# Two of four steps of the first unit's first matrix product in seven products instead of eight

## The chip, the cores and the metric

The kernel runs on one core of one Trainium2 chip. The time is device microseconds of that core, from the first to the last instruction of the program. Five engines work from queues of their own: TensorE (PE, with its weight loads as PEld), VectorE (DVE), ScalarE (ACT), GpSimd (POOL) and SyncE (SP), which mostly issues transfers.

## The reference

```python
kv  = einsum('bhsd,bhse->bhde', k, v)            # 8 batches, 8 heads, 576 rows, 64 columns
out = einsum('bhsd,bhde->bhse', q, kv)
x   = out / sqrt(mean(out**2, -1) + 1e-6) * g_norm   # put together as 4608 x 512
h   = x @ w_in                                   # w_in 512 x 2048
g   = s * max(h, 0)**2 + b
return g @ w_out                                 # w_out 2048 x 512
```

Everything but the two weights is float32. The weights arrive as 64-bit floats and are turned into float32 on the chip.

## The kernel before

The 4608 rows of `x` are worked through in nine **units** of 512 rows. A unit has a first stage (`h` and `g`, called mm1) and a second (`g @ w_out`, called mm2). The attention that makes the `x` of the next unit runs beside them.

**Seven products.** The 2048 columns of `w_in` are taken in four **steps** of 512. Within a step the product of a 512x512 weight block and the unit's 512 columns of `x` transposed is a product of two 2x2 block matrices. Taken plainly it is eight block products. By Winograd's form of Strassen's scheme it is seven, at the price of sums: four of the blocks of `w_in` (`sums_w_in`, two calls `s12` and `s34`, result in `ws`, one in place in `wb`), four of the blocks of `x` (`x_sums`, result in `xs`, shared by all steps of a unit), and additions of the products. `mm1(u, s)` does one step so. The products are named by the PSUM bank and a number: `x1`, `z2`, `x6`, `y7`, `x5`, `x3`, `y4`. `x1`, `x6`, `x5` and `x3` go one after the other into the same bank, each added to what is there. So before `x6` starts, the bank must have been copied out (`keep("r1", ...)`, a ScalarE copy), before `x5` again (`r2`), before `x3` again (`r4`). `z2` plus `r1` is the block `a11` of `h`, `y7` plus `r4` is `a22`, `y4` plus `r2` is `a12`, `x3` gives `a21`. Each is rectified and squared on VectorE (`relu_sq`) and then scaled by `s` and shifted by `b` on ScalarE (`affine`); `a21` is done on ScalarE alone.

**The first unit** takes all four steps plainly (`mm1_plain`, line 656): four slots to a step, each a block of `h` made by eight matmuls of 128x256, into PSUM banks `x` and `y` in turn, two buffers each. `out_of` rectifies the bank's content into a tile of `g` and squares it; the scaling waits in the list `to_scale`, and `scale_g` puts it on ScalarE's queue later. `first_unit` (line 1624) runs the 16 slots; slots 0 to 3 are step 0, and so on. `slots0[0]` and `slots0[1]` are run earlier, between the last pieces of the first attention.

**The conversion of the weights** lies beside these slots. There are 16 tiles: 0 to 7 are `w_in`, 8 to 11 the upper half of `w_out` (`w_up`), 12 to 15 the lower (`w_dn`). A tile comes by DMA into one of three buffers (`w_raw`), takes two passes on ScalarE (`hi`, line 225, and `lo`, line 230) and two on VectorE (`shift`, line 235, and `plus`, line 245). The dictionary `tile_at` says after which slot which tile is converted, `more_at` after which slot a piece of the differences of `w_out`'s halves is formed (`sub_w_out(5, 5, 1, ...)`). All 16 are done by the last slot.

**The second stage of the first unit** is also in seven products, with one difference: product 5 is taken early (`early_5`), with `s1`, the sum of `a21` and `a22` (`g_s1`). Its slots are `x1(0)`, `x1(1)`, `early_5(0)`, `early_5(1)`, `z2(0)`, `z2(1)`, `x6(0)`, and so on; a slot is eight matmuls of 128x256 over the eight blocks of `w_out`, and `z2` is the first that reads `w_dn`. Hung on these slots are: sums of `g` in place (`s2`, `t3`, `s4`), the difference `w_t2` of the halves of `w_out`, the stores of `w_out`'s parts for the later units (`store_w2`), and the load of the next keys, values and queries (`load_kv`, `loads`). The keys and values of batch 1 and `w_t2` go into the three buffers that the weight tiles leave.

**Order.** The order of the instructions on each engine is the order of the program text: nothing is moved by a scheduler. Each engine works through its queue in turn and waits, by semaphores, for operands and for buffers to come free.

Of the kernel before, what the change touches and what calls it, by code (L numbers as in the profile page):

```python
# [16 lines left out]
def kernel(  # L17
# [628 lines left out]
    def relu_sq(t, last=True):  # L646
        nc.vector.scalar_tensor_tensor(t, t, 0.0, t, ALU.max, ALU.mult)  # L647
        if last:
            affine(t)
# [57 lines left out]
    def mm1(u, s):  # L707

        st = {}

        def keep(name, src, tag):
            st[name] = rp.tile([P, 2, TB], FP32, name=name, tag=tag)
            nc.scalar.copy(st[name], src)  # L713

        def x1():
            st["x"] = bank_of("x", "x")
            mm1_product(1, u, s, st["x"], True)
            keep("r1", st["x"], "ra")

        def z2():  # L720
            ps = bank_of("z", "z", 1)
            mm1_product(2, u, s, ps, True)
            t = g_tile("a11", s)
            add(t, ps, st["r1"])
            relu_sq(t)

        def x6():
            mm1_product(6, u, s, st["x"], False)
            keep("r2", st["x"], "rb")

        def y7():
            st["y"] = bank_of("y", "y")
            mm1_product(7, u, s, st["y"], True)

        def x5():
            mm1_product(5, u, s, st["x"], False)
            keep("r4", st["x"], "ra")
            t = g_tile("a22", s)
            add(t, st["y"], st["r4"])
            relu_sq(t)  # L740

        def x3():
            mm1_product(3, u, s, st["x"], False)
            relu_sq_on_act(g_tile("a21", s), st["x"])

        def x3_s1():
            g_tile("s1", s)
            g_s1(s)

        def x3_s3():  # L750
            sub(ga["a21", s], ga["a11", s], ga["a21", s])

        def y4():
            mm1_product(4, u, s, st["y"], False)
            add(g_tile("a12", s), st["y"], st["r2"])

        def y4_square():
            relu_sq(ga["a12", s])

        return dict(  # L760
            x1=x1, z2=z2, x6=x6, y7=y7, x5=x5, x3=x3, x3_s1=x3_s1, x3_s3=x3_s3, y4=y4, y4_square=y4_square,
        )

# [299 lines left out]
    def mm2(u, step=None, side={}):  # L1063
# [148 lines left out]
        def x1(j):  # L1212
            st["x", j] = half(("x", j), "x")
            product(1, j, st["x", j], True)
            part("r1", j, st["x", j])

        def early_5(j):

            ps = half(("w", j), "y")
            product(5, j, ps, True)  # L1220
            nc.scalar.copy(rows("o1", j)[:, HN:], ps)
# [41 lines left out]
        def seq(fn, *more):  # L1263
            def run():
                fn()
                for m in more:
                    m()
            return run
# [11 lines left out]
        if u == 0:  # L1280
            return [
                lambda: x1(0),
                seq(lambda: x1(1), s2),
                lambda: early_5(0),
                lambda: early_5(1),
                lambda: z2(0),
                seq(lambda: z2(1), t3),
                lambda: x6(0),
                seq(lambda: x6(1), s4, t4),
                lambda: y7(0),  # L1290
                lambda: y7(1),
                lambda: x3(0),
                lambda: x3(1),
                lambda: y4(0),
                lambda: y4(1),
            ]
# [231 lines left out]
    gp = ctx.enter_context(tc.tile_pool(name="gp", bufs=NS // 2))  # L1528


    slots0 = [slot for s in range(NS) for slot in mm1_plain(s)]
    turn[0]()
    turn[1]()
    take[0]()
# [82 lines left out]
            for load in load_q(4 * u + 2 * i):  # L1617
                load()  # L1618

    tile_at = {1: 3, 2: 4, 3: 5, 4: 6, 5: 7, 6: 8, 7: 9, 9: 10, 10: 11, 11: 12, 12: 13, 14: 14, 15: 15}  # L1620
    more_at = {8: 8, 9: 9, 12: 10, 13: 11, 14: 12, 15: 13}

    def first_unit():
        for n, slot in enumerate(slots0):
            if n > 1:
                out_of = slot()
                if out_of:
                    out_of()
                if n % 4 == 0:
                    g_s1(n // 4 - 1)  # L1630
            if n in tile_at:
                for step in (hi, lo, shift, plus):
                    step(tile_at[n])
            scale_g()
            if n in more_at:
                more(more_at[n])
        g_s1(NS - 1)

    def x3(a):
        a["x3"]()  # L1640
# [5 lines left out]
    def sides(u, A, B):  # L1646

        first, second = {}, {}  # L1650
        kv = []
        if u in kv_due:
            kv.append(lambda: kv_product(kv_due[u], u > 2))
            kv.append(lambda: used(*((u, "kv", (n, m)) for n in range(NP) for m in range(2))))
        q = {half: [partial(loads, u + 2, half)] for half in range(2)}
        if u == 1:
            for s in range(1, NS):
                first[((0, 1), (0, 3), (1, 1))[s - 1]] = list(sums_w_in(s))
            first.update({
                (1, 3): kv,  # L1660
                (2, 0): [partial(A["turn"], 0), partial(A["turn"], 1)],
                (2, 1): [A["product"]],
                (2, 2): [A["back"]],
                (2, 3): [A["square"]],
                (3, 0): [A["row_sum"]],
                (3, 2): [A["norm"], A["turn_x"]],
                (3, 3): [lambda: [load() for load in load_q(12, rest_on=nc.sync)]],
            })
            return first, second
        if u + 1 == U:  # L1670
            return first, second
        if u == 2:
            first = {
                4: [A["turn"]],
                5: kv,
                8: [A["product"]],
                9: [A["back"], B["turn"]],
                10: [A["square"]],
                11: [A["row_sum"]],
                12: [B["product"]],  # L1680
                13: [A["norm"]],
                14: [A["turn_x"]],
                15: [B["back"], *q[0]],
            }
            second = {
                0: [B["square"]], 1: [B["row_sum"], A["scale"]], 2: [B["norm"]], 3: [B["turn_x"], *q[1]],
                "sums": [B["scale"]],
            }
        else:
            first = {  # L1690
                2: [A["turn"]],
                4: [A["product"], *kv],
                5: [A["back"]],
                6: [A["square"], B["turn"]],
                7: [A["row_sum"]],
                8: [A["norm"]],
                9: [A["turn_x"]],
                10: [B["product"], *q[0]],
                11: [B["back"], A["scale"]],
                12: [B["square"]],  # L1700
                13: [B["row_sum"]],
                14: [B["norm"]],
                15: [B["turn_x"], *q[1]],
            }
            second = {1: [B["scale"]]}
        second[5], second[6] = [[lambda n=n: x_sums(u + 1)[n]()] for n in range(2)]
        return first, second

    for u in range(U):
        A, B = pairs_of(u + 1) if u + 1 < U else (None, None)  # L1710
        if u == 0:
            first_unit()
            second = mm2(0)
        else:
            if u == 1:
                loads(2, 0)
                loads(2, 1)
            first, at_second = sides(u, A, B)
            if u > 1:
                run, last = mm1_deep(u)  # L1720
                second = mm2(u, last, at_second)
                run(lambda n: [fn() for fn in first.get(n, [])], second["early"])
                second["rest"]()
                continue
            steps = [mm1(u, s) for s in range(NS)]
            second = mm2(u)
# [21 lines left out]
        for n, slot in enumerate(second):  # L1748
            slot()
            if u == 0:  # L1750
                if n == 1:
                    for i in range(2):
                        load_kv(1, i, convp, tag="raw", bufs=3)
                    store_w2(1)
                    loads(1, 0)
                    loads(1, 1)
                    store_w2(5)
                elif n == 2:
                    t2 = convp.tile([P, 4 * R * D], FP32, name="w_t2", tag="raw", bufs=3)
                    W2_AT[6] = t2[:, : FC // 2 * HN].rearrange("p (f n) -> p f n", n=HN)  # L1760
                    for i in range(14, 16):
                        more(i)
                    sub_w_out(6, 3, 5)
                    store_w2(3, 2, 6)
            if n == 0 and u > 0:
                x3(steps[-1])
                y4(steps[-1])
            for step in side.get(n, []):
                step()
# [33 lines left out]
```

## Time and profile before

| | |
|---|---|
| time, median of 3 runs | 910.12 us (910.0 to 910.18) |
| profiled span | 908.9 us, TensorE clock 1.000 |
| VectorE, ScalarE, GpSimd busy | 664.5, 356.0, 228.1 us |
| first slots of the first unit | 23.86 us |
| end of its slot 7, start of slot 8 | 53.16 us |
| end of its slot 15, start of `x1(0)` | 80.79 us |
| start of `x6(0)` | 101.51 us |
| start of unit 1 | 135.96 us |

The first unit as busy time of each engine, in stretches of 10 us (PE, PEld, DVE, ACT and POOL with the number of instructions, then the granted clock, the share of the DMA engines and GB/s):

```profile
40.00:50.00 10.00, 10.00 (x48) 8.81 (x47) 8.61 (x12) 8.80 (x11) 0.00 (x0) 1.00 1.01 341
50.00:60.00 10.00, 10.00 (x48) 8.81 (x47) 9.31 (x13) 9.41 (x12) 0.00 (x0) 1.00 0.97 338
60.00:70.00 10.00, 10.00 (x49) 8.79 (x47) 9.66 (x14) 9.37 (x11) 0.00 (x0) 1.00 0.77 258
70.00:80.00 10.00, 10.00 (x48) 8.81 (x47) 8.34 (x12) 7.12 (x9) 0.00 (x0) 1.00 0.88 319
80.00:90.00 10.00, 10.00 (x48) 8.81 (x47) 9.06 (x13) 4.45 (x7) 0.00 (x0) 1.00 0.76 226
90.00:100.00 10.00, 10.00 (x48) 8.79 (x47) 1.42 (x3) 0.74 (x2) 0.00 (x0) 1.00 0.93 243
```

A float32 matmul shows as two records, so a slot of eight matmuls has 16. In a timeline the columns are start, length of the piece, engine, line, operation, output and inputs, shape, number, and in brackets the idle time before it with its releaser. Pieces overlap a little, since the end of one instruction runs into the next.

### The profile page before, as it was taken

The numbers are of one execution on the slowest core, as the hardware profiler recorded it, in microseconds if no ns is written. First come the engines' busy times: TensorE is split into PE (matmuls) and PEld (weight loads), VectorE is DVE, ScalarE is ACT, GpSimd is POOL, SyncE is SP. The second block draws the span as 40 slices with busy tenths as digits, with TensorE's granted clock in tenths as the row PEclk, the third lists the DMA queues.
The fourth block names the chain that finished last, engine by engine and source line by source line (L and its number), as shares of the span: only waits on it lengthen the run. The fifth ranks groups of instructions, "written<-read, shape, count | busy, mean of one in ns | idle before, by whom it ended". The sixth has DMA issues, their size and how long they took to land.

```text
span 908.9 us, 19257 instructions
## 1 busy us (share of the span) xinstructions
PE 897.7 (99%) x7522; PEld 825.3 (91%) x7522; DVE 664.5 (73%) x1230; ACT 356.0 (39%) x600; POOL 228.1 (25%) x432
## 2 busy tenths in 40 slices
PE   7999999999999999999999999999999999999998
PEld 6788888888889998999899998999899989999998
DVE  2898377588567986887678857885878777874686
ACT  2895124531148115630365026701580057104710
POOL 2000016113623232810283036503440300021000
PEclk9999999999999999999999999999999999999999
DMA  9688937339943994379626972598439812891285
GB/s 250 222 305 276 266 82 230 99 88 388 337 138 81 279 336 138 77 239 306 206 70 184 302 254 81 125 305 258 131 88 291 286 37 55 276 303 49 57 256 185
DMA packets 120138, 180.34 MB, mean 198 GB/s; under 512 B 29168, under 2 KB 46320, under 8 KB 120048
## 3 DMA queue, kind: packets, MB, share of 16 engines
q1 hardware_dynamic: 101552, 153.00, 54.2%
q0 software_dynamic: 15040, 23.88, 8.7%
q10 hardware_dynamic: 3456, 2.23, 1.0%
q8 instruction: 60, 0.98, 0.4%
q14 instruction: 30, 0.25, 0.1%
HBM read 153.36 MB, written 25.69 MB: 197 GB/s over the span
## 4 chain that ended last, share of the span: by engine, by line
PE 93%; DVE 4%; DMA 1%; ACT 1%; issue 0%; SPq 0%; DVEq 0%
PE x_ps L91 48%; PE y_ps L91 28%; PE z_ps L91 9%; PE sx_ps L91 4%; PE y_ps L545 2%; DMA kv_sb<-in_v_dram 1%; PE kv_ps L366 1%; PE z_ps L366 1%; DVE xn L578 0%; DVE a L253 0%; PE y_ps L366 0%; DVE sub L253 0%; DVE o L250 0%; DVE xs L253 0%; PE qT_ps L534 0%
## 5 line engine op out<-in xcount | busy, mean ns | idle before, releaser
L1618 POOL DMA_DIRECT2D q_sb<-in_q_dram x256 | 144.0, 571 | 134.8 <-ACT a L652 61.5
L1205 POOL DMA_DIRECT2D out_dram<-o x110 | 55.0, 506 | 397.9 <-issue 160.1
L91 PE MATMUL x_ps<-w_sb,sub 128*128 128x128 f32 x1176 | 148.8, 275 | 0.6 <-DVE r L250 0.6
L91 PEld LDWEIGHTS x_ps<-w_sb,sub 128*128 128x128 f32 x1176 | 139.7, 192 | 0.9 <-DVE r L250 0.9
L644 ACT ACTIVATE a<-a,b_col,s_col 128x512 f32<-128x512 f32 x144 | 116.3, 813 | 29.3 <-DVE a L647 23.2
L91 PE MATMUL x_ps<-xs,ws 128*128 128x256 f32 x512 | 121.4, 380 | 0.1
L91 PE MATMUL y_ps<-xs,wb 128*128 128x256 f32 x512 | 120.8, 381 | 0.0
L91 PEld LDWEIGHTS y_ps<-xs,wb 128*128 128x128 f32 x512 | 94.6, 190 | 12.4 <-issue 0.6
L91 PEld LDWEIGHTS x_ps<-xs,ws 128*128 128x128 f32 x512 | 93.8, 190 | 11.7 <-ACT r L713 0.5
L814 ACT COPY a<-x_ps 128x512 f32<-128x512 f32 x28 | 16.4, 585 | 216.1 <-PE x_ps L91 216.0
L91 PE MATMUL x_ps<-xT,wa 128*128 128x256 f32 x384 | 89.0, 381 | 0.1
L91 PEld LDWEIGHTS x_ps<-xT,wa 128*128 128x128 f32 x384 | 71.3, 190 | 11.0 <-issue 1.5
L250 DVE TENSOR_TENSOR r<-sx_ps,a 128x256 f32<-128x256 f32 x63 | 26.6, 422 | 62.6 <-PE sx_ps L91 62.4
L91 PE MATMUL x_ps<-w_sb,a 128*128 128x128 f32 (+1 forms) x432 | 64.9, 298 | 0.0
L91 PE MATMUL y_ps<-w_sb,a 128*128 128x128 f32 (+1 forms) x416 | 62.1, 295 | 0.0
L91 PEld LDWEIGHTS x_ps<-w_sb,a 128*128 128x128 f32 x432 | 58.9, 191 | 3.3 <-issue 0.4
L91 PEld LDWEIGHTS y_ps<-w_sb,a 128*128 128x128 f32 x416 | 56.1, 192 | 2.1
L250 DVE TENSOR_TENSOR r<-x_ps,o 128x256 f32<-128x256 f32 (+1 forms) x84 | 29.7, 353 | 29.3 <-PE x_ps L91 28.6
L250 DVE TENSOR_TENSOR a<-y_ps,r 128x512 f32<-128x512 f32 x36 | 24.7, 687 | 35.2 <-PE y_ps L91 29.7
L91 PE MATMUL y_ps<-w_sb,sub 128*128 128x128 f32 x392 | 49.5, 275 | 0.0
L253 DVE TENSOR_TENSOR a<-a,a 128x512 f32<-128x512 f32 x72 | 46.8, 684 | 0.4
L91 PE MATMUL z_ps<-w_sb,a 128*128 128x128 f32 (+1 forms) x352 | 46.8, 280 | 0.0
(185 smaller groups left out, 1520.9 us busy)
## 6 DMA issues: line engine op xcount, KB each, us to landing
w_sb<-w SPq DMA_DIRECT2D x385, 256.0 KB, 4.5
w_raw<-in_moe_w_in_dram SPq DMA_DIRECT2D x8, 1024.0 KB, 6.4
w_raw<-in_moe_w_out_dram SPq DMA_DIRECT2D x8, 1024.0 KB, 5.0
w_sb<-w SPq DMA_DIRECT2D x14, 512.0 KB, 8.9
w<-sub POOLq DMA_DIRECT2D x28, 256.0 KB, 6.4
w_sb<-in_k_dram SPq DMA_DIRECT2D x24, 288.0 KB, 4.7
w_sb<-in_v_dram SPq DMA_DIRECT2D x24, 288.0 KB, 5.2
out_dram<-o POOLq DMA_DIRECT2D x92, 64.0 KB, 4.1
```

What stands on the lines that cost most here:

```text
L91: nc.tensor.matmul(o, lhsT=lhsT, rhs=rhs, start=start, stop=stop, skip_group_check=True)
L250: nc.vector.tensor_tensor(out=o, in0=a, in1=b, op=ALU.add)
L253: nc.vector.tensor_tensor(out=o, in0=a, in1=b, op=ALU.subtract)
L366: nc.tensor.matmul(ps[r][(r ^ l) * HB : (r ^ l) * HB + HB, i, :], lhsT=kv[l][0][rows, j, :], rhs=kv[l][1][rows, j, :], start=(j == 0), sto ...
L545: nc.tensor.matmul(ps[l][32 * p : 32 * p + 32, r, lo:hi], lhsT=bd_kv[b % 2][rows, p, at : at + 32], rhs=st["qT"][rows, p, lo:hi], start=Tr ...
L644: nc.scalar.activation(t, t, AF.Identity, scale=s_col, bias=b_col)
L814: nc.scalar.copy(g_tile("a11", s), st["x", s])
L1205: queues[s % 2].dma_start(out=view[b, jj, :, cols], in_=st[name, j][s * w : s * w + w, cols])
L1618: load()
```

## The change

Steps 2 and 3 of the first unit's first stage are done by `mm1` in seven products; steps 0 and 1 stay plain. It takes eight matmuls of 128x256 out of the program. For that the sums of `x` for unit 0 are new, and the sums of `w_in` for steps 2 and 3, which unit 1 formed, are formed in unit 0. To make room on the two engines that convert, tiles 12 to 15 are converted in the second stage, one after each of its first four slots; the loads of keys and values, a store, `w_t2` and the in-place sums `s2` move back with them. The last two products of step 3 run after the second stage's first slot.

```diff
+        def squared(t):
+            relu_sq(t, u > 0)
+            if u == 0:
+                to_scale.append(t)
...
             return [
                 lambda: x1(0),
-                seq(lambda: x1(1), s2),
+                lambda: x1(1),
                 lambda: early_5(0),
-                lambda: early_5(1),
+                seq(lambda: early_5(1), s2),
...
-    slots0 = [slot for s in range(NS) for slot in mm1_plain(s)]
+    slots0 = [slot for s in range(2) for slot in mm1_plain(s)]
...
+            if n == 4:
+                g_s1(0)
+            if n in (1, 2, 3, 4, 5):
+                convert(n + 2)
+            if n == 6:
+                s12, s34 = sums_w_in(2)
+                s12()
+                x_sums(0)[0]()
+            if n == 7:
+                s34()
+                x_sums(0)[1]()
             scale_g()
...
+        a, b = (mm1(0, s) for s in (2, 3))
+        s12, s34 = sums_w_in(3)
+        for step in (
+            [a["x1"], lambda: g_s1(1), partial(convert, 8)],
+            [a["z2"], partial(more, 8)],
+            [a["x6"], s12],
+            [a["y7"], partial(convert, 9)],
+            [a["x5"], s34],
+            [b["x1"], partial(convert, 10)],
+            [a["x3"]],
+            [b["z2"], partial(more, 9)],
+            [a["y4"], a["y4_square"], partial(convert, 11)],
+            [b["x6"], a["x3_s1"]],
+            [b["y7"], partial(more, 10)],
+            [b["x5"], partial(more, 11)],
+        ):
+            for fn in step:
+                fn()
+            scale_g()
+        return b
...
-            for s in range(1, NS):
-                first[((0, 1), (0, 3), (1, 1))[s - 1]] = list(sums_w_in(s))
+            first[0, 1] = list(sums_w_in(1))
...
-                if n == 1:
-                    for i in range(2):
-                        load_kv(1, i, convp, tag="raw", bufs=3)
+                if n == 0:
+                    for name in ("x3", "y4", "y4_square"):
+                        last[name]()
+                    convert(12)
+                    scale_g()
+                    last["x3_s1"]()
                     store_w2(1)
+                elif n == 1:
+                    convert(13)
+                    load_kv(1, 0, convp, tag="raw", bufs=3)
                     loads(1, 0)
                     loads(1, 1)
+                elif n == 2:
+                    convert(14)
+                    load_kv(1, 1, convp, tag="raw", bufs=3)
                     store_w2(5)
-                elif n == 2:
+                elif n == 3:
+                    convert(15)
                     t2 = convp.tile([P, 4 * R * D], FP32, name="w_t2", tag="raw", bufs=3)
                     W2_AT[6] = t2[:, : FC // 2 * HN].rearrange("p (f n) -> p f n", n=HN)
-                    for i in range(14, 16):
-                        more(i)
+                elif n == 4:
                     sub_w_out(6, 3, 5)
                     store_w2(3, 2, 6)
```

More of the change, by code (lines that the diff above doesn't have):

```diff
@@ L724, in z2 @@
             add(t, ps, st["r1"])
-            relu_sq(t)
+            squared(t)
         def x6():
@@ L739, in x5 @@
             add(t, st["y"], st["r4"])
-            relu_sq(t)
+            squared(t)
         def x3():
@@ L757, in y4_square @@
         def y4_square():
-            relu_sq(ga["a12", s])
+            squared(ga["a12", s])
         return dict(
@@ L1618, in loads, with convert @@
                 load()
-    tile_at = {1: 3, 2: 4, 3: 5, 4: 6, 5: 7, 6: 8, 7: 9, 9: 10, 10: 11, 11: 12, 12: 13, 14: 14, 15: 15}
-    more_at = {8: 8, 9: 9, 12: 10, 13: 11, 14: 12, 15: 13}
+    def convert(i):
+        for step in (hi, lo, shift, plus):
+            step(i)
     def first_unit():
@@ L1628, in first_unit @@
                     out_of()
[L1629 to L1633, printed above, removed]
-            scale_g()
-            if n in more_at:
-                more(more_at[n])
-        g_s1(NS - 1)
+            if n == 4:
[9 more added lines that the diff above has]
+                x_sums(0)[1]()
+            scale_g()
+        a, b = (mm1(0, s) for s in (2, 3))
[18 more added lines that the diff above has]
+        return b
     def x3(a):
@@ L1711 @@
         if u == 0:
-            first_unit()
+            last = first_unit()
             second = mm2(0)
```

## The prediction

> **What bounds the kernel.** I read the page's first part first, then the list of waits on TensorE, then the timelines of three engines between 48 and 86 us, where the edited stage runs.
>
> ```profile
> PE 897.7 (99%) x7522; PEld 825.3 (91%) x7522; DVE 664.5 (73%) x1230; ACT 356.0 (39%) x600; POOL 228.1 (25%) x432
> ...
> PE y_ps L91 <- DVE inv L453: 0.4, 1, 0.4
> PE y_ps L91 <- DVE wb L245: 0.3, 1, 0.3
> ```
>
> TensorE is busy for 897.7 of 908.9 us, and the two lines of waits are all that it waited from 28 to 140 us. Nothing later absorbs a shift: a microsecond of TensorE work removed in the first unit ends the kernel a microsecond earlier, a microsecond of new wait a microsecond later.
>
> ```profile
> 49.71 3.62 PE L91 MATMUL y_ps<-xT,wb 128*128 128x256 f32 x16
> 53.16 3.62 PE L91 MATMUL x_ps<-xT,wa 128*128 128x256 f32 x16
> ...
> 53.84 0.68 DVE L691 TENSOR_TENSOR a<-a 128x512 f32<-128x512 f32 x1
> ...
> 56.62 0.68 DVE L686 TENSOR_SCALAR a<-y_ps 128x512 f32<-128x512 f32 x1
> 57.34 0.69 DVE L691 TENSOR_TENSOR a<-a 128x512 f32<-128x512 f32 x1
> ...
> 58.11 0.82 ACT L644 ACTIVATE a<-a,b_col,s_col 128x512 f32<-128x512 f32 x1
> ```
>
> The second PE line is slot 8, the first of the replaced slots. The plain slots are fed in advance: the block that TensorE finished at 53.16 (slot 7) is read by VectorE only at 56.62, squared at 57.34 and scaled on ScalarE at 58.11, 5 us late, and TensorE doesn't care, because it writes another PSUM bank. From 50 to 60 us VectorE is busy for 9.31 and ScalarE for 9.41 of 10 us. So this stage hides a lag of about 5 us on both helpers behind double buffering. In seven products the helpers are on the path:
>
> ```profile
> 141.81 0.81 ACT L644 ACTIVATE a<-a,b_col,s_col 128x512 f32<-128x512 f32 x1 [3.34 <-DVE a L647]
> 142.53 0.56 ACT L713 COPY r<-x_ps 128x512 f32<-128x512 f32 x1
> ...
> 143.15 1.99 PE L91 MATMUL x_ps<-xs,ws 128*128 128x256 f32 x8
> ```
>
> This is the same scheme in unit 1. `x5` adds into the bank that `x6` filled, so the copy `r2` must leave first; the copy stands on ScalarE behind the scaling of `a11`, which waited for VectorE. The copy ends at 143.09 and `x5` starts at 143.15, where 142.92 was due. There, without any conversion, it costs 0.2 us.
>
> [...] the copy, whose operand had long been ready (`x6` ended near 141.2), starts 0.72 us after the scaling ahead of it. [...] here 512 elements take 0.69 us and the shift of 1024 also 0.69 us[...]. [...] the trace, with no gap over 1.6 us after 20 us, shows the clock at 1.00 only[...].
>
> **Prices**, all from these timelines (start to next start): one product of four 128x256 matmuls 1.73 us (135.96, 137.68, 139.41), a plain block 3.455. VectorE: an independent 128x512 operation 0.605, one that waits for its predecessor or reads PSUM 0.7, a conversion 0.82 + 1.14. ScalarE: copy 0.48 (0.59 long), scaling 0.70, each of a conversion's two passes 1.05 (1.16 long), rectify and square 0.62 and 0.66. Hand-over: VectorE to ScalarE 0.08 (58.03 to 58.11), ScalarE to TensorE 0.06, TensorE to ScalarE 0.20 (84.24 to 84.44).
>
> **Part 1, removed.** Two steps of 32 matmuls become 28 each: 8 x 0.432 = **-3.46 us**, all on the path. The sums of `w_in` for steps 2 and 3 leave unit 1 (8 VectorE operations); they ran beside a full TensorE there, so this gains nothing.
>
> **Part 2, the first new wait, `x6` of step 2.** Up to slot 7 both programs are alike. VectorE, in the built order: square of `a21` 53.84, then the four new sums 54.44, 55.14, 55.75, 56.45, then the rectifying of slot 7 at 57.1, its square 57.82 to 58.51. ScalarE's next entry is the scaling of that block, at 58.59; the copy `r1` of the new `x1` stands behind it, 59.29 to 59.88. TensorE finishes `x1` and `z2` at 56.61 and then needs `x6`, which overwrites the bank that `r1` reads: 59.94. **+3.3.**
>
> **Part 3, `x5` of step 2.** TensorE: `x6`, `y7` until 63.40. ScalarE: conversion of tile 8 at 59.77 and 60.82 (ends 61.97), then the scaling of `a11`, then `r2`. VectorE: four more sums from 58.43, `s1` of step 1 at 60.85, shift 61.45, add 62.27, then `a11` 63.41 and its square 64.13 to 64.82. Scaling 64.90, `r2` 65.60 to 66.19, `x5` 66.25. **+2.85.**
>
> **Part 4, step 3.** TensorE: `x5` ends at 67.98, then x1, x3, z2, y4, x6, y7 until 78.34. Between them the copies `r4` (68.18) and `r1` (71.63) are in time. ScalarE from 71.63 has in order: `r1`, tile 10 (two passes), rectify, square and scale `a21`, scale `a11` (waits for VectorE until 76.96, behind tile 10's addition at 74.33), tile 11 (77.66, 78.71), scale `a12` 79.76, and only then `r2`, 80.46 to 81.05. The last `x5` starts at 81.11. **+2.8.**
>
> **Part 5, tiles 12 to 15 and the second stage.** TensorE: x5 until 82.84, `x1(0)` 86.29, `x3`, `y4` 89.75, `x1(1)` 93.20, `early_5` 96.66 and 100.11. `s1` of step 3 is now behind tile 12 on VectorE, ready at about 94.4 and needed by the seventh matmul of `early_5(0)` at 95.8: hidden by the six before it. Then `z2(0)` needs the lower half of `w_out`, and its seventh matmul (102.70) tile 15. ScalarE passes tile 15 only behind the copy of `early_5(1)` (100.31): 100.68 and 101.73, end 102.88. VectorE adds tile 14 at 99.45, then has the four differences of the moved `s2` (100.59 to 103.01), then shift 103.01 and addition 103.83 to 105.05. **+2.4**; without the differences ahead of it still +1.4, which is the low end.
>
> **Part 6, costed at nothing.** `sub_w_out(6, 3, 5)` moves behind `z2(0)`: four operations, from about 106.3 to 109, while `z2(1)` runs until 109.4; `x6(0)` takes them as they come. The second batch of k and v is issued behind tiles 13 and 14 and the eight q loads on the sync queue. The q loads took 10.2 us there, 3.4 of them a wait that tile 13 covers, so the later half goes out at about 104.5 and lands, with 4.2 to 5.8 us as before, by 110.5; its product starts at 113 (105.1 before, plus the shift of 8). The stores of `w_out`'s parts follow; the last that VectorE waits for before `t4` should land near 120, `t4` is due at 122 (114.2 before). Slack of 2 to 3 us in each: no cost, up to +3 if it fails.
>
> **Sum:** -3.46 + 3.3 + 2.85 + 2.8 + 2.4 = +7.9. Forecast 910.1 + 7.9 = **918.0 us**.
>
> **Rivals.** *The gain arrives whole*: the copies get through in time, as in unit 1, where the same scheme lost 0.2 us. That gives 910.1 - 3.5 = 906.7. For it speaks only that unit; against it, that two conversions and a scaling stand ahead of each copy here and that both helpers are over 90% busy. *Only the last tile waits*: the first stage hides everything, z2 doesn't: -3.46 + 2.4, 909.1. It needs ScalarE to be free, which the 9.41 of 10 us denies. *The second stage breaks as well*: late k and v, or late stores that stop VectorE ahead of the attention of unit 1 (+2 to +3), or a halved clock after the 3.3 us gap [...]: 920 to 921. For it speaks that the DMA engines are at 1.0 of their share from 95 to 110 us; against it, the slack above.
>
> **Chances.** Forecast 0.74, whole gain 0.05, only the last tile 0.04, worse 0.17. The four waits are each uncertain by some 0.5 us (1.0 for the last, downwards), so the forecast's own spread is about 915 to 920; with most of the worse case the range is 914.5 to 921.5. Faster 0.05, within 0.2% 0.05 (the second rival and the edge), slower 0.90.
>
> **What would show it.** In the changed trace: four gaps on TensorE, before the second and the third x product of step 2 and the third of step 3, each released by ScalarE's `r` copy, and one within `z2(0)` released by VectorE's addition into `w_dn`. Up to slot 7 nothing moves. The second stage's `x6(0)`, at 101.51 before, starts near 109.4, and the distance from there to the end is unchanged. I am wrong if the copies start within 0.3 us of their product's end, if VectorE's four sums don't stand ahead of slot 7's rectifying, or if `kv_ps` or unit 1's first products wait.

## The result, and the profile after

The changed kernel takes **924.35 us** (median of four runs, 921.99 to 926.07), the kernel before 910.15 us beside it: a ratio of 1.0153, 95% interval [1.013, 1.0176]. The direction was as forecast; the loss is 14.2 us where 7.9 were forecast and at most 11.4 were allowed for.

The first part of the page, and from the list of waits on TensorE three lines, then one of the kernel before:

```profile
PE 902.1 (98%) x7506; PEld 827.8 (90%) x7506; DVE 667.4 (72%) x1234; ACT 360.0 (39%) x606; POOL 227.5 (25%) x432
```

```profile
PE x_ps L91 <- ACT r L718: 6.2, 3, 2.9
PE kv_ps L366 <- DMA kv_sb<-in_v_dram: 4.8, 3, 3.0
PE z_ps L91 <- DVE w_dn L245: 2.2, 1, 2.2
```

```profile
PE kv_ps L366 <- DMA kv_sb<-in_v_dram: 2.4, 3, 1.2
```

TensorE has 16 records less, the eight matmuls, and is nevertheless busy for 4.4 us longer. So it did not only wait more, it also worked more slowly. The lines of waits give the total, the number of times and the longest. The first holds three of the predicted waits, the third the fourth. The second, a wait for keys and values, is the one that the kernel before has too, in three waits of at most 1.2 us; its longest, 3.0 us, is new, and the prediction costed it at nothing.

TensorE's timeline, with the places at which it stopped (the bracket gives the idle time before a line and what ended it):

```profile
52.91 1.89 PE L91 MATMUL x_ps<-xT,wa 128*128 128x256 f32 x8
54.64 1.89 PE L91 MATMUL z_ps<-xT,wa 128*128 128x256 f32 x8
59.39 3.59 PE L91 MATMUL x_ps<-xs,ws 128*128 128x256 f32 x8 [2.86 <-ACT r L718]
62.77 2.02 PE L91 MATMUL y_ps<-xs,wb 128*128 128x256 f32 x8
65.69 1.99 PE L91 MATMUL x_ps<-xs,ws 128*128 128x256 f32 x8 [0.90 <-ACT r L718]
...
80.48 3.48 PE L91 MATMUL x_ps<-xs,ws 128*128 128x256 f32 x8 [2.43 <-ACT r L718]
...
101.06 2.75 PE L91 MATMUL z_ps<-w_dn,a 128*128 128x256 f32 x12
105.97 1.13 PE L91 MATMUL z_ps<-w_dn,a 128*128 128x256 f32 x4 [2.16 <-DVE w_dn L245]
106.94 5.30 PE L91 MATMUL y_ps<-w_dn,a 128*128 128x256 f32 x16
...
115.62 1.28 PE L366 MATMUL kv_ps<-kv_sb 64*64 64x64 f32 x72
119.93 1.30 PE L366 MATMUL kv_ps<-kv_sb 64*64 64x64 f32 x72 [3.02 <-DMA kv_sb<-in_v_dram]
...
151.42 1.89 PE L91 MATMUL x_ps<-xT,wa 128*128 128x256 f32 x8
```

Slot 8 starts at 52.91, about where it did; unit 1 starts at 151.42 instead of 135.96, 15.5 us later, and the whole span is 15.4 us longer. Everything happens between these two lines. The lengths tell as much as the brackets: the products behind the gaps of 2.86 and 2.43 us take 3.59 and 3.48 us instead of 1.89, and `z2(1)`, behind the gap in `z2(0)`, 5.30 instead of 3.62.

The clock, in stretches of 1 us (the length, then PE, PEld, DVE, ACT and POOL busy, the granted clock, the DMA share, GB/s):

```profile
59.00:60.00 1.00, 0.61 (x2) 0.53 (x3) 1.00 (x3) 1.00 (x2) 0.00 (x0) 0.81 0.03 12
60.00:61.00 1.00, 1.00 (x3) 0.80 (x3) 1.00 (x3) 1.00 (x2) 0.00 (x0) 0.50 0.00 0
61.00:62.00 1.00, 1.00 (x4) 0.76 (x3) 0.86 (x3) 0.43 (x1) 0.00 (x0) 0.50 0.00 0
62.00:63.00 1.00, 1.00 (x4) 0.82 (x3) 1.00 (x2) 0.00 (x0) 0.00 (x0) 0.50 0.00 0
63.00:64.00 1.00, 1.00 (x6) 0.87 (x6) 0.96 (x2) 0.00 (x0) 0.00 (x0) 0.98 0.00 0
...
80.00:81.00 1.00, 0.52 (x1) 0.50 (x2) 1.00 (x2) 0.42 (x1) 0.00 (x0) 0.55 0.00 0
...
107.00:108.00 1.00, 1.00 (x5) 0.85 (x4) 0.86 (x2) 0.00 (x0) 0.00 (x0) 0.70 1.21 195
...
121.00:122.00 1.00, 1.00 (x17) 0.82 (x8) 0.00 (x0) 0.66 (x3) 0.00 (x0) 0.53 1.09 314
```

A microsecond of mean clock 0.81 has 0.38 us at half clock, so the slow stretch begins at 59.62; 0.98 gives its end, 63.04: 3.42 us at half speed, 1.71 us lost. Read in the same way, three more slow stretches begin at 80.10, 107.40 and 121.06, each at one of the gaps of 2.16 us or more; at the gap of 0.90 there is none.

The bill, with each product's start against the time at which it was due (0.16 us more than the bracket, each time): `x6` of step 2 3.02, `x5` of step 2 1.06, `x5` of step 3 2.59, `z2` 2.32, the second half of the k-v product 3.17, together 12.2; four stretches at half clock 6.8; the matmuls removed -3.5. That makes 15.5 us, and unit 1 is 15.5 us late. The profile is of the slowest of the four runs, with a mean clock of 0.992; a slow stretch takes about 0.002 off that mean. Two runs with 0.994, one stretch less by that figure, took 924.24 and 924.45; one with 0.998, three stretches less, took 921.99. The first stretch less is worth 1.7 us, the next two 2.4 together, since a slow stretch ahead of a wait for another engine also shortens that wait (as at `x5` of step 2, below). How many gaps bring one differs from run to run.

ScalarE and VectorE ahead of the gaps, to be held against the walk in the prediction:

```profile
58.05 0.81 ACT L644 ACTIVATE a<-a,b_col,s_col 128x512 f32<-128x512 f32 x1 [3.17 <-DVE a L691]
58.77 0.56 ACT L718 COPY r<-x_ps 128x512 f32<-128x512 f32 x1
...
64.36 0.81 ACT L644 ACTIVATE a<-a,b_col,s_col 128x512 f32<-128x512 f32 x1 [2.92 <-DVE a L647]
65.08 0.56 ACT L718 COPY r<-x_ps 128x512 f32<-128x512 f32 x1
...
79.16 0.80 ACT L644 ACTIVATE a<-a,b_col,s_col 128x512 f32<-128x512 f32 x1
79.86 0.56 ACT L718 COPY r<-x_ps 128x512 f32<-128x512 f32 x1
```

```profile
55.99 0.69 DVE L253 TENSOR_TENSOR xs<-xT,xs 128x512 f32<-128x512 f32 x1
56.60 0.68 DVE L686 TENSOR_SCALAR a<-y_ps 128x512 f32<-128x512 f32 x1
57.32 0.69 DVE L691 TENSOR_TENSOR a<-a 128x512 f32<-128x512 f32 x1
```

Each late copy is the second line of a pair. ScalarE stood idle for 3.17 and 2.92 us ahead of the first two pairs: not short of time, but stuck at a scaling whose block VectorE had not squared, with a copy behind it whose operand was ready. The first copy ends at 59.33 (59.88 in the prediction), the second at 65.64 (66.19).

### The profile page after: what moved, and what is told of

Same layout as the page of the kernel before. It is cut to its first block, busy times and chain, and to the rows that moved or that the text cites. A ratio compares the mean times of both kernels' runs of the same rounds, so it can differ in the third digit from the quotient of the medians.

```text
span 924.3 us, 19231 instructions
## 1 busy us (share of the span) xinstructions
PE 902.1 (98%) x7506; PEld 827.8 (90%) x7506; DVE 667.4 (72%) x1234; ACT 360.0 (39%) x606; POOL 227.5 (25%) x432
## 4 chain that ended last, share of the span: by engine, by line
PE 86%; DVE 6%; ACT 3%; DMA 3%; issue 1%; SPq 1%; DVEq 0%; ACTq 0%
PE x_ps L91 45%; PE y_ps L91 24%; PE z_ps L91 9%; PE sx_ps L91 4%; PE y_ps L545 2%; DMA kv_sb<-in_v_dram 2%; ACT w_raw L225 1%; ACT w_raw L230 1%; DMA w_raw<-in_moe_w_in_dram 1%; DVE a L253 1%; PE z_ps L366 1%; PE kv_ps L366 1%; DMA q_sb<-in_q_dram 1%; DVE xs L253 1%; SPq L145 0%
## 5 line engine op out<-in xcount | busy, mean ns | idle before, releaser
L91 PE MATMUL x_ps<-xs,ws 128*128 128x256 f32 x544 | 132.4, 387 | 6.3 <-ACT r L718 6.2
L91 PE MATMUL y_ps<-xs,wb 128*128 128x256 f32 x544 | 128.5, 381 | 0.0
L91 PEld LDWEIGHTS x_ps<-xs,ws 128*128 128x128 f32 x544 | 101.8, 194 | 20.3 <-ACT r L718 7.9
L91 PEld LDWEIGHTS y_ps<-xs,wb 128*128 128x128 f32 x544 | 101.1, 191 | 13.1 <-issue 0.6
L91 PE MATMUL x_ps<-xT,wa 128*128 128x256 f32 x336 | 78.4, 382 | 0.1
L91 PEld LDWEIGHTS x_ps<-xT,wa 128*128 128x128 f32 x336 | 62.3, 190 | 9.6 <-issue 1.3
L250 DVE TENSOR_TENSOR a<-y_ps,r 128x512 f32<-128x512 f32 x40 | 27.5, 688 | 45.8 <-PE y_ps L91 33.7
L647 DVE SCALAR_TENSOR_TENSOR a<-a 128x512 f32<-128x512 f32 x67 | 46.4, 692 | 2.3
```

The lines of the kernel that those rows point to most:

```text
L91: nc.tensor.matmul(o, lhsT=lhsT, rhs=rhs, start=start, stop=stop, skip_group_check=True)
L250: nc.vector.tensor_tensor(out=o, in0=a, in1=b, op=ALU.add)
```

## The experiments

In the expectations, theory A says that the loss is made of waits of TensorE behind the queues of VectorE, ScalarE and the transfers, plus the half clock that a gap brings; the other letters are rivals. All ratios are to the kernel before, run beside them. Some of these kernels spread by more than the clock explains (e5_all takes 912.73 to 917.29 us, and both 912.73 and 916.44 at a mean clock of 0.998). One run of each was traced, so what the others lost beyond it stays open.

| kernel | us | ratio, 95% interval |
|---|---|---|
| changed kernel | 924.35 | 1.0153 [1.013, 1.0176] |
| e1_tiles_only | 915.18 | 1.0056 [1.0041, 1.0071] |
| e2_products_only | 917.47 | 1.0082 [1.0067, 1.0097] |
| e3_fill | 925.15 | 1.0164 [1.0147, 1.0181] |
| e8_more_issue | 918.26 | 1.0083 [1.007, 1.0096] |
| e11_fill8 | 920.27 | 1.0108 [1.0095, 1.0122] |
| e4_copies_first | 920.64 | 1.0118 [1.0092, 1.0145] |
| e6_kv_first | 923.97 | 1.0150 [1.0135, 1.0164] |
| e10_t4_late | 920.01 | 1.0104 [1.009, 1.0117] |
| e7_tiles_early | 917.67 | 1.0077 [1.0064, 1.009] |
| e5_all | 915.80 | 1.0053 [1.004, 1.0066] |
| e9_all2 | 911.15 | 1.0008 [0.9999, 1.0016] |
| e12_all3 | 911.55 | 1.0006 [0.9998, 1.0015] |
| e13_all4 | 907.43 | 0.9968 [0.9956, 0.998] |

### The two halves of the change

**e1_tiles_only** moves the last four tiles and leaves all four steps plain.

```diff
-    slots0 = [slot for s in range(2) for slot in mm1_plain(s)]
+    slots0 = [slot for s in range(NS) for slot in mm1_plain(s)]
...
+    tile_at = {1: 3, 2: 4, 3: 5, 4: 6, 5: 7, 6: 8, 7: 9, 9: 10, 10: 11}
...
                 if n == 0:
                     convert(12)
...
```

> All four steps plain as before; only tiles 12 to 15, the moved s2, the loads of k, v and q and w_t2 stand in the second stage as in the changed kernel. Theory A (waits of tile 15 and of the later k and v, each gap followed by about 3.4 us of half clock): 910.1 + 2.2 (z2) + 3.0 (k and v) + 1.7 to 3.4 (clock) = 917 to 919, with one gap released by the addition into w_dn and one by the load of v. Theory B (all of the loss is in the first stage's seven products): 910 to 911.

915.18 us, +4.9. The gap in `z2` is 2.14 us, the one at the k-v product 2.01; the first stage shows none. So the moved tiles cost these two waits whatever the products do. It is less than the 917 to 919 expected: the second gap is shorter than in the changed kernel, and the clock was 0.997 to 1.000, in the profiled run 1.000 behind both gaps.

**e2_products_only** keeps the seven products, but converts all tiles in or right behind the first stage and leaves the second stage's hangings where they were.

```diff
-            [b["x6"], a["x3_s1"]],
-            [b["y7"], partial(more, 10)],
-            [b["x5"], partial(more, 11)],
+            [b["x6"], a["x3_s1"], partial(convert, 12)],
+            [b["y7"], partial(more, 10), partial(convert, 13)],
+            [b["x5"], partial(more, 11), partial(convert, 14)],
...
                 if n == 0:
...
+                    convert(15)
...
```

> Steps 2 and 3 in seven products as in the changed kernel, but all 16 tiles are converted by the second stage's first slot, and s2, the loads and w_t2 stand where they stood before. Theory A: the gaps before x6 and x5 of step 2 and x5 of step 3 stay (3.0 + 0.9 + 2.6, and up to 1.7 + 1.7 of half clock), those in z2 and in the k-v product go: 910.1 - 3.5 + 9.8 = 916 to 917. Theory B (first stage alone at fault): 924. Theory C (the second stage alone at fault): 906.7.

917.47 us, +7.2, half a microsecond above the 916 to 917 of theory A, with exactly three gaps, 3.04, 0.90 and 2.44, all released by the copy `r`. The clock in the four runs was 0.995 to 0.998. The two halves, +4.9 and +7.2, make 12.1 of the 14.2 us.

### How much is the clock

**e3_fill** puts 26 matmuls of 128x256, whose result nobody reads, ahead of the five gaps, so that TensorE works there instead of waiting.

```diff
...
-            [a["x6"], s12],
+            [lambda: fill(5, bank_t()), a["x6"], s12],
...
-            [b["x5"], partial(more, 11)],
+            [lambda: fill(5, bank_t()), b["x5"], partial(more, 11)],
...
```

> The changed kernel with unused matmuls in the five gaps on TensorE (5 of 128x256 in each of the three x gaps, 4 in z2, 7 in the k-v product: 1.7 to 3.0 us each, no more than the gap), whose results nobody reads. Theory A (a gap brings TensorE's clock down to half for about 3.4 us): clock 1.000 in every run, spread under 1 us; the two half-clock stretches whose loss shortened the wait after them (before x5 of step 2, before the k-v product) give nothing, the two others 1.7 us each: 920.5 to 922.5. Theory D (the clock goes down for another reason, such as the load): the clock stays near 0.994 and the time is 924 or longer by the added matmuls.

A miss: 925.15 us, no faster than the changed kernel. The clock did stay at 1.000 in all four runs, and unit 1 did start 4.9 us earlier than in the changed kernel, at 146.48. But 4.3 us were lost after that, where the two programs are the same. The waits on TensorE name the new places, 3.7 us in all:

```profile
PE z_ps L376 <- issue: 3.0, 2, 1.6
...
PE y_ps L91 <- issue: 0.7, 1, 0.7
```

TensorE stands twice within bursts of small k-v matmuls of later units, and once just behind such a burst, without waiting for anything that the profile shows.

**e8_more_issue** asks whether the mere number of instructions does it: the kernel *before* with 26 matmuls of 64x64 added ahead of slot 2, whose result nobody reads.

```diff
     def first_unit():
         for n, slot in enumerate(slots0):
+            if n == 2:
+                ps = ps_t.tile([P, 2, D], FP32, name="more_ps", tag="t")
+                for _ in range(26):
+                    nc.tensor.matmul(ps[:HB, 0, :], lhsT=ident[:HB, :D], rhs=ident[:HB, :D], start=True, stop=True)
```

> The kernel before with 26 more unused matmuls of 64x64 on TensorE beside slot 2 (0.02 us each by the k-v product's 144 in 2.3 us, so 0.4 us of work). With the filled gaps 4.3 us went astray after unit 1 had begun, in the bursts of small matmuls of the later k-v products. Theory J (the number of instructions ahead of these bursts decides how long they idle, and the fill changed it): 911 to 915, with idle time put to issue in the later k-v products. Theory K (it was something else in the filled kernel): 910.3 to 910.8.

918.26 us. Unit 1 starts 3.5 us later, of which the added matmuls are 3.24 (0.06 us a record, where 0.02 had been expected), and a further 4.3 us come after it, most of them again within bursts of small k-v matmuls:

```profile
PE z_ps L366 <- issue: 3.5, 3, 1.6
```

That is theory J, with the added work priced too low. So the 4.3 us that e3_fill lost late need not come from the change: 26 more matmuls ahead of the bursts bring them to the kernel before as well.

**e11_fill8** therefore fills with eight matmuls of 128x512 only, just enough to keep each gap under 2 us; nobody reads their result either.

```diff
...
-            [a["x6"], s12],
+            [partial(fill, 2), a["x6"], s12],
...
-            [a["x5"], s34],
+            [partial(fill, 1), a["x5"], s34],
...
```

> The changed kernel with eight unused matmuls of 128x512 (0.86 us each) in its gaps: two, one and two in the x gaps, one in z2, two in the k-v product. That is the number of matmuls that the change took out, so the later small products should idle as in the kernel before. Theory A (half clock follows a gap, and eats time of its own in the second and the last of the four places): clock 0.998 or more, 919.5 to 922. Theory D (the clock has no part in the loss): 924 to 925.

920.27 us, 4.1 less than the changed kernel, although nothing comes earlier on any other engine. Gaps of 0.7 to 1.7 us are left, the clock is 0.999 to 1.000 in all runs, and the four runs lie within 0.6 us instead of 4.1. In the median, the half clock is 4.1 of the 14.2 us.

### The single waits

**e4_copies_first** puts copies of the bank ahead of conversions and scalings on ScalarE.

```diff
...
-            [a["x1"], lambda: g_s1(1), partial(convert, 8)],
-            [a["z2"], partial(more, 8)],
-            [a["x6"], s12],
+            [a["x1"], scale_g, lambda: g_s1(1), partial(convert, 8)],
+            [a["z2"], partial(more, 8), a["x6"], s12],
...
```

> The changed kernel with ScalarE's order changed in three places: the scaling of slot 7's block after the copy r1, the scaling of a11 after r2, and in step 3 the scalings of a11 and a12 and tile 11's conversion after r2. Theory A (the copies are late because of what stands ahead of them in ScalarE's queue): the gaps before x6 and x5 of step 2 shrink from 3.0 + 0.9 to about 0.4, with 1.4 before y7, which then waits for VectorE's sums of x; the gap of step 3 goes, and two half-clock stretches with them: about 916.5. Theory E (VectorE's load sets these gaps whatever ScalarE's order): within 1 us of 924.

920.64 us: half of what was expected. The gaps ahead of `x6` and both `x5` are gone, which shows that what stood ahead of the copy made them: one scaling in step 2, two scalings and tile 11 in step 3. But the next copy, `r4`, now stands behind the scaling instead, and with its gap comes the half clock:

```profile
67.43 3.68 PE L91 MATMUL x_ps<-xT,ws 128*128 128x256 f32 x8 [2.37 <-ACT r L718]
```

`y7` waits 1.17 us for VectorE's last sum of `x`. Moving one entry of a full queue handed the wait to the next.

**e6_kv_first** issues the second half of the keys and values ahead of the eight q loads.

```diff
                     load_kv(1, 0, convp, tag="raw", bufs=3)
-                    loads(1, 0)
-                    loads(1, 1)
...
                     load_kv(1, 1, convp, tag="raw", bufs=3)
+                    loads(1, 0)
+                    loads(1, 1)
                     store_w2(5)
```

> The changed kernel with one edit: the eight loads of q are issued after the second half of the keys and values instead of before it. Theory A (that half is late because it stands behind the q loads in the sync queue, which wait in turn for earlier transfers): the gap of 3.0 us in the k-v product goes and a half-clock stretch with it: 919.5 to 921.5. Theory H (the DMA engines are full in this stretch, so the order of issue changes nothing): 923.5 to 925.

A miss: 923.97 us. The k-v product no longer waits, but 2.9 us turn up a little later. VectorE's and TensorE's timelines:

```profile
126.89 2.50 DVE L253 TENSOR_TENSOR w_dn<-w_dn,w_t 128x512 f32<-128x512 f32 x4 [5.28 <-DMA w<-w_dn]
```

```profile
130.41 1.97 PE L534 MATMUL qT_ps<-ident,q_sb 128*128 128x128 f32 x8 [2.89 <-DVE q_sb L557]
```

`t4` overwrites a part of `w_dn` that the late stores still read; the shuffle of q for TensorE's transposes stands behind it on VectorE.

**e10_t4_late** is e6_kv_first with `t4` two slots later.

```diff
...
-                seq(lambda: x6(1), s4, t4),
+                seq(lambda: x6(1), s4),
                 lambda: y7(0),
-                lambda: y7(1),
+                seq(lambda: y7(1), t4),
...
```

> The kernel with keys and values ahead of the queries, where the k-v gap went but t4's difference on VectorE waited 5.3 us for the store of the part it overwrites, and held the transposes that TensorE's next transposes waited for (2.9 us). One more edit: t4 two slots later, behind y7(1). Theory L (the transfers that were moved back are one queue, and shortening one wait there lengthens the next until the last consumer has slack): that gap goes as well, 919 to 921.5. Theory M (VectorE is late by itself): the gap of 2 to 3 us before the transposes stays, 923 or more.

920.01 us: the 2.9 us gap is gone, 1.02 us are left at the product of line 545. The transfers' part of the loss is about 4 us with the half clock behind it, and it takes both edits to get it.

**e7_tiles_early** converts tiles 12 to 15 one place earlier each, and both halves of the k-v load with them; the second stays behind the q loads.

```diff
-            [b["x5"], partial(more, 11)],
+            [b["x5"], partial(more, 11), partial(convert, 12)],
...
                 if n == 0:
...
-                    convert(12)
+                    convert(13)
...
```

> The changed kernel with one edit: tiles 12 to 15 are converted one slot earlier, the loads that need their buffers with them. Theory A: the gap in z2 goes (2.2 us, up to 1.7 of half clock), the one in the k-v product shrinks by about 1.2: 918.5 to 921. Rival I (the tiles aren't late because of their place, but because ScalarE has no time for them): the gap in z2 stays above 1.5 us and the time above 923.

917.67 us: the gaps in `z2` and at the k-v product are both gone, a little better than expected. One slot is enough for the second stage.

### A version without waits

Four kernels put these orders together, each to take away what the last one left.

**e5_all** has tiles early, k and v ahead of q, copies ahead of scalings or conversions, the sums of `x` four slots earlier and those of `w_in` for step 2 one or two.

```diff
...
         for step in (
-            [a["x1"], lambda: g_s1(1), partial(convert, 8)],
+            [a["x1"], partial(convert, 8), scale_g],
...
-            [a["x6"], s12],
-            [a["y7"], partial(convert, 9)],
+            [a["x6"], s12, partial(convert, 9), scale_g],
+            [a["y7"]],
...
```

> The same seven products with all the named waits taken away by order alone: the sums of x beside plain slots 2 and 3, the first sums of w_in beside slot 4, each copy r ahead of the scalings and conversions that it stood behind, tiles 12 to 15 one place earlier, keys and values ahead of the queries. Theory A (the loss is these waits and the half clock after them, nothing else): no gap over 0.5 us on TensorE between 30 and 140 us, clock 1.000, and the removed 3.5 us come out: 906.7 to 908.5. Theory G (the two helpers can't carry seven products and the conversion together in any order): 912 or more, with gaps released by VectorE.

915.80 us, above what was expected: VectorE was 3 us behind at slots 6 and 7, and gaps of 2.31 and 1.49 us ahead of `x6` and the last `x5` were left, with half clock in all runs (0.995 to 0.998). The profile is of the fastest of the six.

**e9_all2** moves the second pair of these sums of `x` back to slot 6 and tile 11 behind `y4`, scales the blocks of the last plain slots behind `r1` or `r2`, and has `t4` late.

```diff
...
-            [a["x1"], partial(convert, 8), scale_g],
+            [a["x1"], partial(convert, 8), scale_two],
...
-            [b["z2"], partial(convert, 11)],
-            [a["y4"], a["y4_square"]],
+            [b["z2"]],
+            [a["y4"], a["y4_square"], partial(convert, 11)],
...
```

> The version with all waits ordered away, mended after its first run. There VectorE came 3 us late to slots 6 and 7, since the early sums weren't absorbed by its idle time, and the copy r1 stood behind two scalings of slots 5 and 6; the second r2 needed the buffer that y4's addition reads, behind tile 11. Now the later two sums of x come after slot 6's square, the scalings of slots 5 to 7 after r1 or r2, tile 11 after y4, and the difference t4 of w_out, which had waited for a store, two slots later. Theory A: no gap over 0.6 us before the second stage, 907 to 909.5. Theory G (the helpers can't carry it): again 912 or more.

911.15 us, level with the kernel before and above the 907 to 909.5 expected. Gaps of 1.03, 1.69 and 1.02 us are left; the clock is 0.999 to 1.000.

**e12_all3** takes these three away.

```diff
...
-            [a["x5"], s34],
-            [b["x1"], partial(convert, 10), scale_g, partial(more, 8), lambda: g_s1(1)],
+            [a["x5"], partial(scale, 1), s34],
+            [partial(convert, 10)],
+            [b["x1"], scale_g, partial(more, 8), lambda: g_s1(1)],
...
```

> e9_all2 with its three remaining waits taken away by order alone: in step 2 the scaling of a11 stands behind the copy r4 (as it came first, x3 waited 1.03 us); tile 10 goes ahead of b's x1 and tile 11 behind b's r2 (before b's last x5 1.69 us were waited); the difference t4 is put before x3(0), behind the row sums of the next attention (1.02 us at the product of L545). Theory A (the program's loss is nothing but these waits, the eight matmuls are worth 3.46 us): the gaps are each under 0.4 us, unit 1 starts near 133.5, and the kernel takes 907 to 908.5 us, the first version below the kernel before. Theory G (each shift of one wait makes another, because both helpers have no spare time in this stage): new gaps of 1 us or more, 910 or above.

911.55 us: a miss. One long gap is left, ahead of the same last `x5` as in e9_all2, but with a new cause. TensorE's timeline and ScalarE's:

```profile
74.70 3.65 PE L91 MATMUL x_ps<-xs,ws 128*128 128x256 f32 x8 [2.25 <-ACT r L718]
```

```profile
74.06 0.59 ACT L718 COPY r<-x_ps 128x512 f32<-128x512 f32 x1 [3.55 <-DVE a L250]
```

The copy has ScalarE to itself and waits for its own buffer, which the addition behind `y4` reads; that addition stood on VectorE behind tile 10. And the gap of 2.25 us cost the half clock in most runs: nine of thirteen took 911.33 to 911.86 at 0.997 or 0.998, the other four 910.00 to 910.36 at 0.999 or more. One gap costs 2.3 us, or nearly 4 with the half clock: the medians of the two groups, 911.70 and 910.14, are 1.56 us apart.

**e13_all4** leaves tile 10's ScalarE passes where they are and puts its VectorE half, and what followed it, behind that addition.

```diff
...
-            [partial(convert, 10)],
-            [b["x1"], scale_g, partial(more, 8), lambda: g_s1(1)],
+            [partial(hi, 10), partial(lo, 10)],
+            [b["x1"], scale_g],
...
-            [b["x6"], partial(convert, 11), scale_g, a["x3_s1"], partial(more, 9), partial(more, 10)],
+            [b["x6"], partial(shift, 10), partial(plus, 10), partial(convert, 11), scale_g],
             [b["y7"]],
-            [b["x5"], partial(convert, 12), scale_g, partial(more, 11)],
+            [b["x5"], partial(more, 8), lambda: g_s1(1), a["x3_s1"], partial(more, 9)],
+            [partial(convert, 12), scale_g, partial(more, 10), partial(more, 11)],
...
```

> e12_all3, where b's last x5 waited 2.25 us for the copy r2, which waited for its buffer, which is read by the addition behind y4, which stood on VectorE behind tile 10, a difference and a sum. Here the two ScalarE passes of tile 10 keep their place, but its two VectorE operations, tile 11, the difference and the sum go behind that addition (2 + 0.6 + 0.6 us of VectorE work less ahead of the copy). Theory A (the loss is nothing but the waits): the copy ends near 71.5, b's x5 starts without a gap, no stretch of half clock, unit 1 near 133.5, kernel 907 to 908.5 us. Theory G (the stage is full: the wait turns up elsewhere): a new gap of 1 us or more, most likely before x1(0)'s seventh matmul (tile 11, due at 76.6) or in z2 (tile 15), 910 or above.

**907.43 us**, 0.32% below the kernel before ([0.9956, 0.998]), as theory A has it. VectorE's timeline, then TensorE's:

```profile
70.32 0.68 DVE L250 TENSOR_TENSOR a<-y_ps,r 128x512 f32<-128x512 f32 x1
71.03 0.69 DVE L647 SCALAR_TENSOR_TENSOR a<-a 128x512 f32<-128x512 f32 x1
71.64 0.69 DVE L235 TENSOR_SCALAR w_up<-w_raw 128x1024 uint32<-128x1024 uint32 x1
```

```profile
70.76 1.89 PE L91 MATMUL y_ps<-xs,wb 128*128 128x256 f32 x8
72.48 1.89 PE L91 MATMUL x_ps<-xs,ws 128*128 128x256 f32 x8
74.21 3.62 PE L91 MATMUL x_ps<-w_up,a 128*128 128x256 f32 x16
...
132.83 1.89 PE L91 MATMUL x_ps<-xT,wa 128*128 128x256 f32 x8
```

The addition comes at 70.32, ahead of tile 10; the last `x5` follows `y7` without a bracket; unit 1 starts at 132.83, 3.13 us before the kernel before. The arithmetic and the number of busy instructions on each engine are those of the changed kernel: between 924.35 and 907.43 lies the order alone.

## Why the prediction was wrong, point by point

**The bound: right.** TensorE's time passes through undiminished. Unit 1 starts 15.5 us later, the span is 15.4 longer; in e13_all4 both are 3.1 us shorter.

**Part 1, -3.46: right in size**, but only e13_all4 could show it. Of the 3.46 us, 2.8 arrive in the medians (3.1 between the two traced runs, 0.3 of them ahead of slot 8); the rest goes in four short stops of steps 2 and 3, 0.07 to 0.32 us each.

**Parts 2 to 4, the three copies: right in mechanism.** The prediction has +3.3, +2.85, +2.8; the products were late by 3.02, 1.06 and 2.59. The second differs by its own cause: `x6` ran at half clock and ended 1.7 us later, so that less was left to wait for `r2`. In e6_kv_first's profile, where this stretch didn't come, the bracket is 2.58. e4_copies_first shows that it is what stands ahead of the copy, since reordering moved each wait. In the changed kernel the ready copies started 0.72, 0.72 and 0.70 us after the scalings ahead of them.

**Part 5, tile 15: right.** +2.4, measured 2.32 late.

**Part 6, costed at nothing: the first failed step.** A waiting `kv_ps` was named as a sign of being wrong, at up to +3, but the walk of the queue said that it would not wait. It put the issue of the second half of k and v at 104.5 and its landing at 110.5. SyncE's queue:

```profile
98.11 2.66 SPq L107 DMA_DIRECT2D kv_sb<-in_k_dram  x1
100.81 1.69 SPq L107 DMA_DIRECT2D kv_sb<-in_v_dram  x1
102.55 9.26 SPq L145 DMA_DIRECT2D q_sb<-in_q_dram  x8
111.91 0.57 SPq L107 DMA_DIRECT2D kv_sb<-in_k_dram  x1
112.52 0.47 SPq L107 DMA_DIRECT2D kv_sb<-in_v_dram  x1
```

The second half went out at 111.9 and 112.5 and its product could start at 119.93. The first term that failed is the start of the q loads: the first half of k could go only when tile 13 had left its buffer, at 98.1, and k and v then took 4.4 us to issue, so q began at 102.55. The second is their length: 6.8 us were reckoned, with the wait in them covered by tile 13, and 9.26 were needed. The third is the way from issue to landing, 7.4 us where 5.8 was the most allowed for: the price came from a stretch in which the DMA engines were at 0.76 of their share (80 to 90 us before), and from 112 to 120 us they now were at 0.98. So the data came 9.4 us after the 110.5 of the prediction; the product itself was due 3.8 us later than forecast (116.8, not 113), the slack took 2.5, and about 3 us of wait remain. For the stores the slack held; e6_kv_first shows that it wouldn't have after the next edit.

**The clock: the second failed step.** The prediction had the half clock as one possibility in a rival of 0.17, once, behind a gap of 3.3 us. In the trace of the changed kernel it came four times, behind gaps of 2.16 to 3.02 us.

Between 25 and 895 us all fifteen traces hold 15 slow stretches, each at a gap on TensorE of 2.16 to 3.59 us; in the changed kernel they begin between 0.38 us ahead of the gap's end and 1.43 us behind it. Eight other gaps of 2 us or more brought none: 2.44, 2.58 and 2.89 us ahead of `x5` and `x6` in e6_kv_first, where these products took 1.99 us each (3.59 at half clock in the changed kernel), 2.01 and 2.14 in e1_tiles_only, and the 2.14 in `z2` in e4_copies_first, e6_kv_first and e10_t4_late. No shorter gap brought one. So the length of a gap alone does not decide; what else does is not shown, since no run moved a gap in time and left its length as it was.

e11_fill8 prices the clock: 4.1 us in the median.

With the two terms added, 7.9 + 3.0 + 4.1 = 15.0 us against 14.2 measured.

**The rivals.** The gain whole was what the order of e13_all4 brings, not this one. "The second stage breaks as well" named both failures, but each as an alternative and once; they came together, and the clock up to four times. The range had no room for that.

## What to carry to other kernels

Price a gap on TensorE by its length and, from about 2 us on, by the half clock that can follow it: here up to 1.7 us more, behind 15 of the 23 gaps of 2.0 to 3.6 us in the traces. Eight filling matmuls, which left gaps of 0.7 to 1.7 us, were enough to keep the clock at 0.999 to 1.000. When a load is moved behind others on the queue, walk that queue from its first entry, with what each entry waits for, as carefully as an engine's. When the helpers are nearly full, count what stands ahead of each copy that frees a bank, the operations that free the copy's own buffer too, and split a long conversion so that its parts can stand where each engine has time.

## What had not been expected of the hardware

More TensorE instructions ahead of bursts of 64x64 matmuls can bring idle time in those bursts that no wait explains: 4.3 us both in e3_fill (18 matmuls more than the kernel before) and in e8_more_issue (26 more), and none that shows in e11_fill8 (as many as the kernel before) or in the changed kernel (eight fewer). The cause stays open; the runs vary only the count.

The 26 added matmuls of 64x64 took 0.06 us a record, 0.12 us each, 3.24 us in all. The 144 records of the k-v product, of the same size, took 2.33 us in the kernel before, 0.016 a record. The added ones all use one place of the inputs and of the bank; those of the k-v product go through four combinations of halves, and in the trace of the kernel before four records of a later k-v product start within 0.02 us of each other (535.20 to 535.22). That this is the reason is not shown, but to price the added ones by the k-v product, as the expectation of e8_more_issue did, gave far too little.
